# Two loads of v moved from GpSimd's DMA queue to SyncE's, each cut into 119 and 9 rows

## The chip, the cores and the metric

The kernel runs on one core of a Trainium2 chip. The metric is device time in microseconds (us), the median of several runs; lower is better. The profile comes from one further execution of the same program.

## The reference

The kernel computes two layers in one launch. The first is attention with a forget gate, over 8 batches and 8 heads, with 576 positions and 64 channels a head. The second mixes the result along the sequence in the frequency domain.

```python
# attention, for each batch and head
cum    = cumsum(log(clip(f, 0.0001, 1)))
scores = q @ k.T / sqrt(64) + cum[:, None] - cum[None, :]      # causal
x      = softmax(scores) @ v                                   # -> [8, 576, 512]
# spectral mix: 64 low modes, for each a complex 512 x 512 weight
X = rfft(x, axis=1)
Yr, Yi = Xr @ w_r - Xi @ w_i,  Xr @ w_i + Xi @ w_r             # per mode m < 64
u   = x + irfft(Y)
out = u + relu(u @ w_ch)
```

The two weights `w_r` and `w_i` are [64, 512, 512] in float32 and make up most of what is read: 134.2 MB of the 163.7 MB that the profile counts as read from HBM.

## The kernel before

**Attention stage.** Heads are taken in pairs of one batch: 32 pairs, and the list `pairs` runs over the batches inside each pair of heads. The loop at L552 runs over `i` from 0 to 33. In iteration `i` it issues loads for later pairs, computes the scores of pair `i`, and finishes the attention of pair `i - 1` and the transform (`dft`) of pair `i - 2`. From iteration 10 on it also does a part of the spectral product (`spec_early`).

**Spectral stage.** The loop at L716 runs over `u` from 0 to 15, four modes at a time. For each `u` it multiplies with the remaining weight tiles (`spec_mms`, matmuls at L194), rearranges the result, and in the later turns folds finished modes back into x (`fold_modes`, `fold`). The last `u` is multiplied in `spec_cols` (L211). Then come twenty output blocks (`bases`, `rest`) with stores from SyncE (L860 and L865).

**Loads.** Almost every load is issued by GpSimd, in program order, onto one DMA queue (q0 in the profile):

- `load_qk` (L109): q and k of a pair, cast from float32 to bf16 by the DMA, two transfers.
- `load_v` (L119): v of a pair, 128 rows of 2304 bytes in float32, with no cast, into a tile `vt` from a pool of four buffers. Row p of the tile holds nine positions of one head.
- `issue_w` (L156 and L165): weight tiles, cast to bf16, in transfers of 512 KB or 1024 KB as written. In the attention loop they are issued in halves (`issue_half`), and a pool of seven buffers (`wpool`) holds them.

In iteration `i` GpSimd issues q and k of pair `i + 4`, half a weight tile, v of pair `i + 3`, and in most iterations another half. SyncE's queue (q1 in the profile) carries only f and v of the first three pairs at the start, and the output stores at the end. The tile `vt` is read by one VectorE instruction, `scale_v` (L372), which multiplies it by the decay weights `wn`; `scale_v(i + 1)` stands near the end of iteration `i`. With four buffers, the load of v of pair 8 waits for `scale_v(4)`, and that of pair 16 for `scale_v(12)`.

The instructions themselves are fetched by DMA while the kernel runs. These fetches are the queues q8 and q14 in the profile.

Of the kernel before, what the change touches and what calls it, by code (L numbers as in the profile page):

```python
# [23 lines left out]
def kernel(  # L24
# [11 lines left out]
    nc = tc.nc  # L36
# [66 lines left out]
    def load_qk(i):  # L103
        g, b = pairs[i]
        qk = qkpool.tile([128, 2, S], BF16, tag="qk", name="qk")
        st[i]["qk"] = qk

        for n, src in enumerate((q, k)):
            nc.gpsimd.dma_start(  # L109
                qk[64 * n : 64 * n + 64, :, :],  # L110
                src[b, 2 * g : 2 * g + 2, :, :].rearrange("h (p r) d -> p h (r d)", p=64),
            )

    def load_v(i, eng=None):

        g, b = pairs[i]
        vt = vpool.tile([128, 9, Dh], F32, tag="vt", name="vt")
        st[i]["vt"] = vt
        (eng or nc.gpsimd).dma_start(  # L119
            vt[:].rearrange("p r d -> p (r d)"),  # L120
            v[b, 2 * g : 2 * g + 2, :, :].rearrange("h (c r) d -> (h c) (r d)", r=9),
        )


    early = [(u, 0) for u in range(NU)] + [(u, 1) for u in range(NX)]
# [48 lines left out]
    def issue_half():  # L174
        issue_w(whalf[0])
        whalf[0] ^= 1
# [91 lines left out]
    def setup_cum():  # L268
        nc.vector.tensor_tensor_scan(cum[:, 0:S], ones1, lf, 0.0, ALU.mult, ALU.add)
        rref = ssb.tile([BH, 1], F32, name="rref")  # L270
        nc.vector.tensor_copy(rref[:], cum[:, 256:257])
        nc.vector.tensor_scalar(cum[:, 0:S], cum[:, 0:S], rref[:], None, ALU.subtract)
        nc.vector.tensor_copy(cum[:, S : 2 * S], cum[:, 0:S])
        nc.vector.tensor_copy(cum[:, 2 * S : 2 * S + 64], cum[:, 512:576])
# [14 lines left out]
    def setup_wn(r0, r1):  # L289
        cpn = psM.tile([128, 5, BH], F32, tag="m", name="cpn")  # L290
        for r in range(r0, r1):
            nc.tensor.transpose(
                cpn[:, r - r0, :], cum[:, r : 2 * S : 9], ident_f[:BH, :BH]
            )
        for hp in range(2):
            half = slice(64 * hp, 64 * hp + 64)
            nc.scalar.activation(
                wn[half, :, r0:r1],
                cpn[half, 0 : r1 - r0, hp:BH:2].rearrange("p r w -> p w r"),
                ACT.Exp,  # L300
                scale=-1.0,
            )

    def setup_small():
        nc.vector.tensor_scalar(trimask[:], m_f[:], s_f[:, 0:1], None, ALU.is_ge)
        nc.vector.memset(tri4[:], 0.0)
        nc.vector.tensor_copy(tri4[0:64, 0, :], trimask[0:64, 0:64])
        nc.vector.tensor_copy(tri4[64:128, 1, :], trimask[64:128, 64:128])
# [37 lines left out]
    def trans(i, part):  # L346

        qk = st[i]["qk"]
        if part == 0:
            st[i]["T"] = qtkt.tile([128, 2, S], BF16, tag="T", name="qkT")  # L350
        r0, r1 = (0, 5) if part == 0 else (5, 9)
        tp = psM.tile([128, 5, 2, 64], BF16, tag="m", name="tp")
        for r in range(r0, r1):
            for hp in range(2):
                nc.tensor.transpose(  # L355
                    tp[64 * hp : 64 * hp + 64, r - r0, :, :].rearrange("p n c -> p (n c)"),
                    qk[:, hp, r * 64 : r * 64 + 64],
                    ident_bf[:, :],
                )
        nc.vector.tensor_copy(  # L360
            st[i]["T"][:].rearrange("p n (c r) -> p n c r", r=9)[:, :, :, r0:r1],
            tp[:, 0 : r1 - r0, :, :].rearrange("p r n c -> p n c r"),
        )
# [12 lines left out]
    def turn_v(i):  # L376

        tv = psM.tile([128, 9, 64], BF16, tag="m", name="tv")
        for r in range(9):
            for hp in range(2):  # L380
                sl = slice(64 * hp, 64 * hp + 64)
                nc.tensor.transpose(tv[sl, r, :], st[i]["vn"][sl, r, :], ident_bf[sl, sl])  # L382
        st[i]["vT"] = vTpool.tile([128, S], BF16, tag="vT", name="vT")
        nc.vector.tensor_copy(  # L384
            st[i]["vT"][:].rearrange("p (c r) -> p c r", r=9), tv[:].rearrange("p r c -> p c r")
        )
# [25 lines left out]
    def scores(i, T):  # L412

        QT, KT = st[i]["T"][:, 0, :], st[i]["T"][:, 1, :]
        if T == 0:
            st[i]["et"] = epool.tile([128, 3, 2, 512], BF16, tag="et", name="et")
            st[i]["e4"] = epool.tile([128, 64], BF16, tag="e4", name="e4")
            st[i]["m4"] = epool.tile([128, 2, 64], BF16, tag="m4", name="m4")
        if T == 3:
            ps = psM.tile([128, 64], F32, tag="m", name="s4")  # L420
            for hp in range(2):
                sl = slice(64 * hp, 64 * hp + 64)
                nc.tensor.matmul(
                    ps[sl, :], lhsT=KT[sl, 512:576], rhs=QT[sl, 512:576], start=True, stop=True
                )
            nc.scalar.activation(st[i]["e4"][:], ps[:], ACT.Exp, scale=scale)
            return
        ps = psS.tile([128, 2, 512], F32, tag="S", name="sps")
        for jb, i0, n, c in SPANS[T]:
            for hp in range(2):  # L430
                sl = slice(64 * hp, 64 * hp + 64)
                nc.tensor.matmul(  # L432
                    ps[:, hp, c : c + n],
                    lhsT=KT[sl, jb * 128 : jb * 128 + 128],
                    rhs=QT[sl, i0 : i0 + n],
                    start=True,
                    stop=True,
                )
        nc.scalar.activation(st[i]["et"][:, T, :, :], ps[:], ACT.Exp, scale=scale)  # L439
# [29 lines left out]
    def av(i, sb):  # L469
        if sb in (0, 3):  # L470
            st[i]["pav"] = psV.tile([128, 3, 2, Dh + 1], F32, tag="av", name="pav")
        pav, vs = st[i]["pav"], st[i]["vs"]
        Ms = SBLK[sb]
        for hp in range(2):
            for jb in range(sb + 1):
                rhs = vs[:, 8, :] if jb == 4 else vs[:, 2 * jb + hp, :]
                nc.tensor.matmul(  # L477
                    pav[:Ms, sb % 3, hp, :],
                    lhsT=eblk(i, hp, jb, sb),
                    rhs=rhs,  # L480
                    start=(jb == 0),
                    stop=(jb == sb),
                )
# [62 lines left out]
            nc.vector.tensor_tensor(y, A[:], y, ALU.add)  # L546

    less = (3, 6, 9, 12, 15)
    trans(0, 0)
    trans(0, 1)  # L550
    spec_done = 0
    for i in range(NPAIR + 2):  # L552
        live = i < NPAIR
        if i + 4 < NPAIR:
            load_qk(i + 4)
        issue_half()
        if i + 3 < NPAIR:
            load_v(i + 3)
        if i not in less:
            issue_half()  # L560
        prev = i - 1 if 1 <= i <= NPAIR else None
        if live:
            scores(i, 0)
        if i == 0:
            setup_cum()
            setup_small()
        if prev is not None:
            av(prev, 0)
            av(prev, 1)
        if live:  # L570
            scores(i, 1)
        if 0 < i < NPAIR:
            turn_v(i)
        if prev is not None:
            av(prev, 2)
            norm(prev, 0)
        if i + 1 < NPAIR:
            trans(i + 1, 0)
        if live:
            scores(i, 2)  # L580
            if i == 0:
                setup_wn(0, 5)
                setup_wn(5, 9)
                scale_v(0)
                setup_w()
                turn_v(0)
            mask(i, 0)
        if prev is not None:
            av(prev, 3)
        if i + 1 < NPAIR:  # L590
            trans(i + 1, 1)
        if live:
            scores(i, 3)
            back_v(i)
        if prev is not None:
            av(prev, 4)
            norm(prev, 1)
        if live:
            mask(i, 1)
        if i + 1 < NPAIR:  # L600
            scale_v(i + 1)
        if i == 1:
            setup_basis()
        if 10 <= i < 14:
            spec_early(*early[spec_done])
            spec_done += 1
        if i >= 2:
            dft(i - 2)
        if i == 2:
            setup_late()  # L610
        if 3 <= i < 3 + NSB:
            setup_bi(i - 3)
        if i == 3 + NSB:
            setup_bi4(0, 512)
        if i == 4 + NSB:
            setup_bi4(512, 64)
        if i >= 10:
            spec_early(*early[spec_done])
            spec_done += 1
# [3 lines left out]
    with ExitStack() as bctx:  # L623
# [8 lines left out]
        with ExitStack() as mctx:  # L632
# [83 lines left out]
            for u in range(NU):  # L716
# [4 lines left out]
                for dc in range(first, NEB - 1 if last else NEB):  # L721
# [3 lines left out]
                    if u >= NF and dc < 3:  # L725
                        b = 2 * (u - NF) + dc - 1
# [169 lines left out]
```

## Time and profile before

| What | Value |
|---|---|
| Median of 3 runs | 441.06 us (440.43 to 441.65) |
| Time of the profiled execution | 442.7 us |
| Its span, first to last instruction | 440.7 us |
| Mean granted TensorE clock | 0.936 of full speed |
| Busy: TensorE, VectorE, ScalarE, GpSimd | 344.5, 268.4, 233.3, 129.7 us |
| Read from HBM, written | 163.73 MB, 9.44 MB |
| DMA queue of GpSimd (q0) | 62800 packets, 85.64 MB as written |
| DMA queue of SyncE (q1) | 5504 packets, 10.47 MB |

The span is what the profile's rows add up to; 2.0 us of the profiled execution's time lie outside it. Busy time of an engine is an average over stages with different limits, so a change in one stage is read from that stage.

A transfer is shared out over the core's 16 DMA engines, and each of them tells of its own share's landing; whoever waits for the transfer waits for all of them. The trace keeps these landings, and it keeps every packet with its queue, start, duration and size, but not the number of the DMA engine that moved it.

### The profile page before, as it was taken

The page shows a single profiled execution, that of the slowest core. Times are in us where ns is not written, and L with a number is a line of the kernel's source. Part 1 is how long each engine was busy: PE and PEld are TensorE (multiplying, and loading weights), DVE is VectorE, ACT ScalarE, POOL GpSimd, SP SyncE. Part 2 cuts the span into 40 slices and gives each one's busy share as a digit, 9 for nine tenths or more (in the row PEclk, how much of TensorE's full clock was granted, in tenths as well). Part 3 has the DMA queues.
Part 4 walks back from the last instruction along what each step waited for, and adds up shares of the span by engine and source line. Part 5 has one row for each costly group of instructions (what it writes and reads, how often), then busy time and mean ns, then how long its engine had stood idle before and what let it go on. Part 6 is the DMA issues. An engine that isn't in the chain of part 4 may idle for free.

```text
span 440.7 us, 10287 instructions
## 1 busy us (share of the span) xinstructions
PE 344.5 (78%) x4295; PEld 189.9 (43%) x4305; DVE 268.4 (61%) x641; ACT 233.3 (53%) x355; POOL 129.7 (29%) x199
## 2 busy tenths in 40 slices
PE   1678878889889889898893694797885788979993
PEld 0455555555555565555551241343442233325331
DVE  6678888777887778888871221223231356635885
ACT  4567678778787665665640031132222355734673
POOL 6544444453454444444222111012211221100000
PEclk9999999999999999999997598599989699969997
DMA  8999999999999999999999999999999999992698
GB/s 190 205 234 221 230 220 231 232 228 227 231 231 222 231 222 229 221 230 224 232 212 212 212 212 212 212 212 212 211 212 210 211 210 210 210 210 53 219 347 294
DMA packets 68349, 96.75 MB, mean 220 GB/s; under 512 B 3536, under 2 KB 45008, under 8 KB 68304
## 3 DMA queue, kind: packets, MB, share of 16 engines
q0 software_dynamic: 62800, 85.64, 104.9%
q1 hardware_dynamic: 5504, 10.47, 6.8%
q8 instruction: 33, 0.54, 0.4%
q14 instruction: 12, 0.10, 0.1%
HBM read 163.73 MB, written 9.44 MB: 393 GB/s over the span
## 4 chain that ended last, share of the span: by engine, by line
DMA 39%; PE 34%; DVE 19%; ACT 3%; issue 3%; POOL 1%; DVEq 0%; POOLq 0%; ACTq 0%
DMA w<-in_moe_w_i_dram 22%; DMA w<-in_moe_w_r_dram 15%; DVE vT L384 5%; DVE x_all L492 4%; DVE qkT L360 4%; PE pav L477 4%; PE A L194 4%; PE sps L432 3%; PE tv L382 3%; PE pd L521 3%; PE vp L393 2%; PE U L785 2%; DMA qk<-in_k_dram 2%; PE Z L785 2%; DVE vn L372 2%
## 5 line engine op out<-in xcount | busy, mean ns | idle before, releaser
L439 ACT ACTIVATE et<-sps 128x1024 bf16<-128x1024 f32 x96 | 96.0, 1050 | 12.6 <-PE sps L432 10.2
L744 DVE TENSOR_TENSOR Yb<-A,yx 128x512 bf16<-128x512 f32 x15 | 10.4, 692 | 67.6 <-PE A L194 67.6
L477 PE MATMUL pav<-vs,et 128*128 128x65 bf16 (+1 forms) x896 | 51.2, 197 | 0.2 <-DVE vn L372 0.2
L360 DVE COPY qkT<-tp 128x640 bf16<-128x640 bf16 x64 | 48.8, 763 | 3.1 <-PE tp L355 3.0
L477 PEld LDWEIGHTS <-et 128*128 128x128 bf16 (+1 forms) x896 | 36.5, 102 | 17.2 <-issue 13.3
L194 PE MATMUL A<-w,XP 128*16 128x512 bf16 (+1 forms) x240 | 22.6, 457 | 27.1 <-DMA w<-in_moe_w_i_dram 15.6
L660 PE MATMUL pxw<-wch,xT 128*128 128x512 bf16 (+1 forms) x152 | 39.1, 403 | 1.0 <-DVE xT L651 0.4
L432 PE MATMUL sps<-qkT 64*128 64x512 bf16 (+4 forms) x320 | 38.9, 306 | 1.1 <-DVE qkT L360 1.1
L492 DVE TENSOR_TENSOR x_all<-pav,rcp 128x384 bf16<-128x384 f32 (+2 forms) x96 | 36.2, 377 | 3.3
L355 PE MATMUL tp<-ident_bf,qk 128*64 128x128 bf16 x576 | 29.3, 231 | 9.9 <-DMA qk<-in_k_dram 9.9
L384 DVE COPY vT<-tv 128x576 bf16<-128x576 bf16 x32 | 24.2, 757 | 19.3 <-PE tv L382 19.3
L667 ACT CAST XW<-pxw 128x512 bf16<-128x512 f32 (+1 forms) x15 | 8.8, 585 | 48.3 <-PE pxw L660 48.3
L165 POOL DMA_DIRECT2D w<-in_moe_w_r_dram x16 | 11.9, 743 | 70.1 <-PE A L194 56.7
L404 ACT COPY vs<-vp 128x576 bf16<-128x576 bf16 x32 | 20.5, 640 | 21.4 <-PE vp L400 21.4
L156 POOL DMA_DIRECT2D w<-in_moe_w_r_dram x27 | 20.5, 759 | 38.5 <-PE A L194 8.6
L667 ACT CAST yx<-pxw 128x512 bf16<-128x512 f32 (+1 forms) x25 | 14.6, 585 | 32.4 <-PE pxw L660 32.4
L165 POOL DMA_DIRECT2D w<-in_moe_w_i_dram x19 | 13.3, 700 | 55.8 <-PE A L194 26.1
L109 POOL DMA_DIRECT2D qk<-in_q_dram x32 | 19.7, 614 | 33.8 <-PE tp L355 7.8
L706 ACT CAST x_all<-pu 128x512 bf16<-128x512 f32 (+1 forms) x40 | 23.4, 584 | 9.0 <-PE pu L705 8.0
L491 DVE RECIPROCAL rcp<-pav 128x6 f32<-128x6 f32 (+2 forms) x96 | 16.2, 169 | 16.3 <-PE pav L477 16.1
L156 POOL DMA_DIRECT2D w<-in_moe_w_i_dram x27 | 20.4, 756 | 17.5 <-DMA w<-in_moe_w_i_dram 8.2
L109 POOL DMA_DIRECT2D qk<-in_k_dram x32 | 19.4, 605 | 20.2 <-DMA w<-in_moe_w_r_dram 6.5
(134 smaller groups left out, 666.5 us busy)
## 6 DMA issues: line engine op xcount, KB each, us to landing
w<-in_moe_w_r_dram POOLq DMA_DIRECT2D x16, 1024.0 KB, 29.6
w<-in_moe_w_i_dram POOLq DMA_DIRECT2D x15, 1024.0 KB, 32.1
w<-in_moe_w_r_dram POOLq DMA_DIRECT2D x27, 512.0 KB, 11.1
w<-in_moe_w_i_dram POOLq DMA_DIRECT2D x27, 512.0 KB, 12.5
vt<-in_v_dram POOLq DMA_DIRECT2D x29, 288.0 KB, 10.6
out_dram<-o_sb SPq DMA_DIRECT2D x16, 512.0 KB, 3.4
qk<-in_q_dram POOLq DMA_DIRECT2D x32, 144.0 KB, 10.7
qk<-in_k_dram POOLq DMA_DIRECT2D x32, 144.0 KB, 10.8
```

The costliest lines, as they stand in the source:

```text
L109: nc.gpsimd.dma_start(qk[64 * n : 64 * n + 64, :, :], src[b, 2 * g : 2 * g + 2, :, :].rearrange("h (p r) d -> p h (r d)", p=64),)
L156: nc.gpsimd.dma_start(w8[:, t, :, :], src[4 * u : 4 * u + 4, dc * 128 : (dc + 1) * 128, :].rearrange("m p e -> p m e"),)
L165: nc.gpsimd.dma_start(w8[:, j : j + step, :, :].rearrange("p m r e -> p m (r e)"), src[m : m + step, 256:512, :].rearrange("m (p r) e -> p ...
L194: nc.tensor.matmul(A[32 * j : 32 * j + M, :], lhsT=lhsT, rhs=rhs, start=st_, stop=sp_)
L355: nc.tensor.transpose(tp[64 * hp : 64 * hp + 64, r - r0, :, :].rearrange("p n c -> p (n c)"), qk[:, hp, r * 64 : r * 64 + 64], ident_bf[:, :],
L360: nc.vector.tensor_copy(st[i]["T"][:].rearrange("p n (c r) -> p n c r", r=9)[:, :, :, r0:r1], tp[:, 0 : r1 - r0, :, :].rearrange("p r n c ...
L384: nc.vector.tensor_copy(st[i]["vT"][:].rearrange("p (c r) -> p c r", r=9), tv[:].rearrange("p r c -> p c r"))
L432: nc.tensor.matmul(ps[:, hp, c : c + n], lhsT=KT[sl, jb * 128 : jb * 128 + 128], rhs=QT[sl, i0 : i0 + n], start=True, stop=True,)
L439: nc.scalar.activation(st[i]["et"][:, T, :, :], ps[:], ACT.Exp, scale=scale)
L477: nc.tensor.matmul(pav[:Ms, sb % 3, hp, :], lhsT=eblk(i, hp, jb, sb), rhs=rhs, start=(jb == 0), stop=(jb == sb),)
L492: nc.vector.tensor_tensor(x_all[:ns, g, b, lo:hi, :].rearrange("p s (h d) -> p s h d", h=2), pav[:ns, lo % 3 : lo % 3 + n, :, 0:Dh], _stri ...
L660: nc.tensor.matmul(pxw[:Ms, :], lhsT=xT[:, eb, sb * 128 : sb * 128 + Ms], rhs=wch[:, eb, :], start=(eb == 0), stop=(eb == NEB - 1),)
```

## The change

In iterations 5 and 13, v of pairs 8 and 16 (the ninth and the seventeenth) is loaded by two transfers on SyncE's queue, of rows 0 to 118 and of rows 119 to 127, instead of one transfer of 128 rows on GpSimd's queue. The other 27 loads of v in the loop stay as they are. The bytes, the tile and its reader are the same.

```diff
-    def load_v(i, eng=None):
+    def load_v(i, eng=None, parts=((0, 128),)):
 
         g, b = pairs[i]
         vt = vpool.tile([128, 9, Dh], F32, tag="vt", name="vt")
         st[i]["vt"] = vt
-        (eng or nc.gpsimd).dma_start(
-            vt[:].rearrange("p r d -> p (r d)"),
-            v[b, 2 * g : 2 * g + 2, :, :].rearrange("h (c r) d -> (h c) (r d)", r=9),
-        )
+        rows = v[b, 2 * g : 2 * g + 2, :, :].rearrange("h (c r) d -> (h c) (r d)", r=9)
+        for p0, p1 in parts:
+            (eng or nc.gpsimd).dma_start(
+                vt[p0:p1, :, :].rearrange("p r d -> p (r d)"), rows[p0:p1, :]
+            )
...
     less = (3, 6, 9, 12, 15)
+    uneven = (8, 16)
...
         if i + 3 < NPAIR:
-            load_v(i + 3)
+            if i + 3 in uneven:
+                load_v(i + 3, nc.sync, ((0, 119), (119, 128)))
+            else:
+                load_v(i + 3)
```

## The prediction

> **What bounds the kernel now.** I read the slices and queues of the page first, then the chain, then TensorE's timeline where the chain changes hands, and last the rows of `vt`.
>
> ```profile
> DMA  8999999999999999999999999999999999992698
> ...
> q0 software_dynamic: 62800, 85.64, 104.9%
> q1 hardware_dynamic: 5504, 10.47, 6.8%
> q8 instruction: 33, 0.54, 0.4%
> q14 instruction: 12, 0.10, 0.1%
> ...
> DMA 39%; PE 34%; DVE 19%; ACT 3%; issue 3%; POOL 1%; DVEq 0%; POOLq 0%; ACTq 0%
> ```
>
> The DMA engines are over 90% busy in every slice up to about 397 us, whatever the compute engines do, and DMA holds the largest share of the chain. So the loads run as one stream, and the kernel ends a fixed tail after that stream. The chain's order of time (rows from 309 us, three of them) and TensorE's timeline show where the tail begins:
>
> ```profile
> 309.21 33.62 DMA w<-in_moe_w_i_dram
> ...
> 359.39 28.41 DMA w<-in_moe_w_i_dram
> 387.84 1.09 PE A L194 x7
> ```
>
> ```profile
> 385.26 0.65 PE L194 MATMUL A<-w,XP 128*16 128x512 bf16 x8
> 387.84 1.06 PE L194 MATMUL A<-w,XP 128*16 128x512 bf16 x8 [1.93 <-DMA w<-in_moe_w_i_dram]
> ```
>
> The chain goes over for good from DMA to TensorE at 387.84 us, when the last weight tile of `u` = 14 has landed (387.80). TensorE had waited 1.93 us for it. The later tiles land before TensorE comes to them (the last at 402.90, used at 405.03), so the end lies 52.9 us after this one landing.
>
> A landing means the last of 16 shares. The landing records of this tile, one per DMA engine, lie at these lags after the first, in us: 0, 0.09, 0.38, 0.50, 0.51, 1.64, 2.45, 2.84, 2.98, 3.91, 4.02, 4.16, 4.86, 4.89, 4.96, 5.92. Each engine gets an equal share of every transfer before, so the lags are work of other kinds. The instruction fetches are that work: q8 has 33 of 16 KB, each one packet on one engine, of 0.89 to 0.98 us (one longer), and where one falls after 220 us, the lag of one engine grows by about 1 us and the others stay (at the landing after the fetch of 255.7 us the last lag goes from 5.02 to 5.97). The fetches come round to the same engine every eighth time (223.0 and 399.6 us), and the eight engines that they visit are, as far as the records can be followed, the eight slowest in the list. Smaller fetches (q14, 0.32 us) explain part of the middle. Fast engines do not wait for slow ones: the queue is 10 to 30 us deep (median from issue to landing 10.6 us for v, 29.6 us for the large weight tiles). The kernel is therefore bound by its slowest DMA engine, 5.92 us behind the fastest and 1 us behind the next.
>
> **The change, part by part.**
>
> *Removed from GpSimd's queue:* two transfers. The rows of v:
>
> ```profile
> L372 DVE TENSOR_TENSOR vn<-vt,wn x32: 741/743/758, 17.6 to 221.7; 128x576 bf16<-128x576 f32 x32
> L119 POOL DMA_DIRECT2D vt<-in_v_dram x29: 557/562/578, 16.4 to 207.9; - x29
> L119 SPq DMA_DIRECT2D vt<-in_v_dram x3: 432/432/560, 1.4 to 2.5; - x3
> ```
>
> GpSimd saves 2 x 0.562 us of issue. That is worth nothing: what follows in its order is queued 1.7 to 23 us before the first engine gets to it. Every DMA engine loses its share of 8 rows, which takes 0.73 us (step from one landing to the next on the first engine, 0.71 to 0.75 where nothing disturbs it). Twice: 1.46 us.
>
> *Added to SyncE's queue:* four transfers of about 0.43 us of issue each, on an engine with nothing between 3 us and the stores at 410.5 us; nothing is queued behind them that matters. They wait for the buffer: `scale_v(4)` ends at 42.9 us and `scale_v(12)` at 94.3 us, against issues on GpSimd at 52.1 and 104.5 us. So v comes some 10 us earlier than now and is read at 67.6 and 120.8 us; a landing even 10 us slower than now is hidden. VectorE's two `scale_v` wait for two landings each instead of one, at a cost of 0.02 us (its one separate semaphore step takes 21 ns), within gaps of that engine.
>
> *The shares.* The trace shows only transfers of 64 and 128 rows on SyncE's queue, and each lands in 16 steps. 119 is 7 x 17 and 9 is 3 x 3, so neither divides by 16. Equal shares mean at most seven engines of 17 rows, and nine of one row. A row of 2304 bytes on this queue takes 0.093 us alone (median packet). Back to back, packets start 0.089 us apart. The seven engines then carry 18 x 0.089 = 1.60 us in place of 0.73, which is +0.87 us each time and +1.74 in all. Engines that get nothing gain 1.46; those with one row gain 1.46 - 0.18 = 1.28. Mixing two queues on an engine may cost more: in the first 10 us, where both run, the same packets often take 0.106 us, 0.013 more. 36 of these are +0.47, so the seven's price lies between +1.74 and +2.21. I take 1.74, from rows in their steady run, and keep the other for the range.
>
> The trace does not say which seven. The Trainium skill, page "DMA: Bandwidth & Descriptors", section "Why a DMA increments its semaphore by 16 and not by 1", says that on this queue the largest count up to 16 that divides the row dimension is used, on the lowest-numbered engines. That gives engines 0 to 6 for the 119 rows; no run so far shows a transfer that doesn't divide by 16.
>
> A hint from packet records: an output store at 413.27 us coincides with the last q8 fetch. Its first packets start on 15 engines 0 to 154 ns after the first, at nearly the same distances as in the store before; the one missing is, in that store, about the twelfth of 16 to start. If shares are handed out in engine order, the fetched engines are not the first seven. This is weak, but it is all there is.
>
> *The sum.* If the seven are among the engines without q8 fetches, the slowest goes from 5.92 to 5.92 - 1.46 = 4.46, and the highest of the others from 2.84 to 2.84 + 1.74 = 4.58. The new last share is at 4.46 to 4.58: 1.34 to 1.46 us earlier, less than TensorE's wait of 1.93, so the whole tail moves. The span becomes 440.7 - 1.4 = 439.3, and the profiled execution 442.7 - 1.4 = 441.3. That execution lies 1.6 us above the median of the runs; I carry the difference over, which gives 441.06 - 1.4 = 439.7 us (0.3% less). With mixing, 2.84 + 2.21 = 5.05, and the gain is 0.87.
>
> **Rivals.**
>
> *The seven include the laggards (slower).* Place: the landing at 387.80. If the engine at 5.92 is among the seven, it goes to 5.92 + 1.74 to 2.21, and the end moves to 442.8 to 443.3 us. If only the one at 4.96 is, 4.96 + 1.74 = 6.70, and the end is 0.8 later, 441.8. It decides as soon as any engine above 5.92 - 1.74 = 4.18 is loaded, and four are. For it: eight of 16 engines are visited, and seven drawn blindly would nearly always hit one of the four. Against: the hint above, and fetches that keep to eight engines look like a fixed half.
>
> *The shares aren't equal but spread over all 16,* 7 or 8 rows each. Then the queue changes and no engine's load does: 8 x 0.089 = 0.71 against 0.73. 441.0 us. All 16 landings of 64 and 128 rows speak for it as much as for the forecast.
>
> *Few engines.* Were all 119 rows on one, 119 x 0.089 = 10.6 us each time, 21.2 in all on one engine, less 1.46: even the fastest would end 13.8 us after the slowest now, near 455 us. Nothing in the trace speaks for it.
>
> The Trainium skill has a rule against the change: the same page, "Rules for kernel authors", asks for a dimension that is a multiple of 16 outermost, so that all 16 engines work. By it the transfer itself takes longer, 17 rows or 1.5 us for 0.73; here that is hidden 10 us deep, and only the sum per engine counts.
>
> **How the numbers follow.** A measurement of this kernel tells about 0.3% (1.3 us) from no change. Equal shares on engines without q8 fetches: 0.67, of which 0.53 beyond 0.3% and 0.14 below (mixing). Laggards among the seven: 0.25, of which 0.22 beyond. Spread: 0.05, same. Few engines: 0.03, slower. That is faster 0.53, same 0.22, slower 0.25. The prediction is 439.7. The range starts at the gain of 1.46 with 0.4 for the spread of runs, 439.2, and reaches up into the laggard case, 442.9; on its own the likeliest case has 439.2 to 440.4.
>
> **What would show it.** Right: q1 gains 256 rows (0.59 MB) and one landing packet for each share, so 5504 + 256 + 32 = 5792 packets if seven and nine engines take part and 5824 if all 16 do; the lags of the last tiles spread over 4.5 us instead of 5.9; the chain's hand-over to TensorE comes near 386.4 with a wait of about 0.5 us. Wrong: a hand-over after 387.8 with a spread of 6.7 or more (laggards loaded), or a spread of 5.9 unchanged (spread shares). A landing of v later than 67.6 or 120.8 us would refute that its time is hidden.

## The result, and the profile after

The changed kernel takes 444.12 us (median of 6 runs, 442.81 to 445.41), the kernel before 441.0 us in the same job (median of 6, 440.0 to 443.26). The ratio is 1.0062, 95% interval 1.0039 to 1.0086: 2.7 us slower by this ratio (the medians lie 3.1 us apart), where the forecast was 1.4 us faster. A second job (run `e11_after_again` below) gave 1.0060 (1.0032 to 1.0088).

The page of the changed kernel, the slices, queues and shares of the chain:

```profile
DMA  8999999999999999999999999999999999993697
...
q0 software_dynamic: 62640, 85.05, 104.7%
q1 hardware_dynamic: 5792, 11.06, 7.2%
q8 instruction: 34, 0.56, 0.5%
q14 instruction: 12, 0.10, 0.1%
...
DMA 39%; PE 36%; DVE 17%; ACT 4%; issue 2%; POOL 1%; DVEq 0%; POOLq 0%; ACTq 0%
```

The DMA engines are as busy as before. q1 has the 5792 packets that the prediction gave for shares on seven and on nine engines, and not the 5824 of shares on all 16. The Trainium skill's rule for that (page "DMA: Bandwidth & Descriptors", section "Why a DMA increments its semaphore by 16 and not by 1": the largest number up to 16 that divides the rows) agrees with this count.

The rows of v, and the chain where it goes over from DMA to TensorE, with TensorE's timeline there:

```profile
L373 DVE TENSOR_TENSOR vn<-vt,wn x32: 741/743/759, 17.2 to 223.7; 128x576 bf16<-128x576 f32 x32
L121 POOL DMA_DIRECT2D vt<-in_v_dram x27: 562/562/571, 16.5 to 210.7; - x27
L121 SPq DMA_DIRECT2D vt<-in_v_dram x7: 270/350/560, 1.4 to 96.6; - x7
```

```profile
311.90 33.64 DMA w<-in_moe_w_i_dram
...
361.69 28.82 DMA w<-in_moe_w_i_dram
390.55 0.67 PE A L195 x8
```

```profile
389.12 0.64 PE L195 MATMUL A<-w,XP 128*16 128x512 bf16 x8
390.55 0.65 PE L195 MATMUL A<-w,XP 128*16 128x512 bf16 x8 [0.79 <-DMA w<-in_moe_w_i_dram]
```

The hand-over is at 390.55 us; it was at 387.84 and was expected at 386.4. The last weight tile lands from 399.52 us (first of 16 shares) to 405.54 (last share), before from 396.93 to 402.90. So both ends of the stream came 2.6 us later, and the spread stayed at 6.0 us.

The span of this execution grew by 1.0 us alone (441.7 for 440.7). In it TensorE had a higher granted clock behind the hand-over, which fits a shorter tail. Two rows of the table of stretches, first of the changed kernel, then of the kernel before (columns: stretch, its length, TensorE busy, granted clock, DMA share, GB/s):

```profile
388.00:400.00 12.00, 9.89 (x90) 1.00 1.14 208
```

```profile
388.00:400.00 12.00, 10.91 (x79) 0.73 1.03 190
```

The clock was 1.00 in the one and 0.73 in the other, and the tail from the hand-over to the end took 51.2 us in the one and 52.9 in the other. One execution's span can therefore hide a shift of the stream; I read shifts from the landings, and times from the medians.

### The profile page after: what moved, and what is told of

The parts are those of the page before. It is cut to its first block, busy times and chain, and to the rows that moved or that the text cites. A ratio compares the mean times of both kernels' runs of the same rounds, so it can differ in the third digit from the quotient of the medians.

```text
span 441.7 us, 10310 instructions
## 1 busy us (share of the span) xinstructions
PE 351.4 (80%) x4305; PEld 192.8 (44%) x4305; DVE 269.4 (61%) x641; ACT 233.2 (53%) x355; POOL 128.6 (29%) x197
## 3 DMA queue, kind: packets, MB, share of 16 engines
q1 hardware_dynamic: 5792, 11.06, 7.2%
## 4 chain that ended last, share of the span: by engine, by line
DMA 39%; PE 36%; DVE 17%; ACT 4%; issue 2%; POOL 1%; DVEq 0%; POOLq 0%; ACTq 0%
DMA w<-in_moe_w_i_dram 22%; DMA w<-in_moe_w_r_dram 15%; PE pav L478 5%; DVE vT L385 4%; DVE qkT L361 4%; DVE x_all L493 4%; PE A L195 4%; PE sps L433 3%; PE tv L383 3%; PE pd L522 3%; PE vp L394 2%; PE U L790 2%; DMA qk<-in_k_dram 2%; PE Z L790 2%; ACT e L427 1%
## 5 line engine op out<-in xcount | busy, mean ns | idle before, releaser
L478 PE MATMUL pav<-vs,et 128*128 128x65 bf16 (+1 forms) x896 | 52.7, 200 | 0.2 <-DVE vn L373 0.2
L478 PEld LDWEIGHTS <-et 128*128 128x128 bf16 (+1 forms) x896 | 37.6, 104 | 18.3 <-issue 13.8
L665 PE MATMUL pxw<-wch,xT 128*128 128x512 bf16 (+1 forms) x160 | 41.9, 419 | 0.0
L433 PE MATMUL sps<-qkT 64*128 64x512 bf16 (+4 forms) x320 | 40.5, 317 | 1.1 <-DVE qkT L361 1.1
L356 PE MATMUL tp<-ident_bf,qk 128*64 128x128 bf16 x576 | 30.3, 237 | 9.6 <-DMA qk<-in_k_dram 9.6
L166 POOL DMA_DIRECT2D w<-in_moe_w_i_dram x19 | 13.3, 700 | 57.0 <-PE A L195 26.2
L665 PEld LDWEIGHTS <-xT 128*128 128x128 bf16 (+1 forms) x160 | 15.8, 108 | 22.7 <-issue 9.2
```

What stands on the lines that cost most here:

```text
L166: nc.gpsimd.dma_start(w8[:, j : j + step, :, :].rearrange("p m r e -> p m (r e)"), src[m : m + step, 256:512, :].rearrange("m (p r) e -> p ...
L356: nc.tensor.transpose(tp[64 * hp : 64 * hp + 64, r - r0, :, :].rearrange("p n c -> p (n c)"), qk[:, hp, r * 64 : r * 64 + 64], ident_bf[:, :],
L433: nc.tensor.matmul(ps[:, hp, c : c + n], lhsT=KT[sl, jb * 128 : jb * 128 + 128], rhs=QT[sl, i0 : i0 + n], start=True, stop=True,)
L478: nc.tensor.matmul(pav[:Ms, sb % 3, hp, :], lhsT=eblk(i, hp, jb, sb), rhs=rhs, start=(jb == 0), stop=(jb == sb),)
L665: nc.tensor.matmul(pxw[:Ms, :], lhsT=xT[:, eb, sb * 128 : sb * 128 + Ms], rhs=wch[:, eb, :], start=(eb == 0), stop=(eb == NEB - 1),)
```

## The experiments

Four ideas were held against each other. *Engine sum:* the end goes with the DMA engine that has most to do, and one of the engines far behind is among the seven loaded. *Window:* GpSimd issues a transfer only after the eighth one before it has landed whole, so late shares hold up all engines. *Queue:* v on SyncE's queue comes too early or costs as such. *The forecast's sum:* the seven are engines without large instruction fetches, and nobody waits for them. ("Lane theory" in the texts on record is the engine sum in its first form; the "price theory" of the last run is the engine sum with the row prices of the traces.)

The window came from the trace. In the landing records, GpSimd's transfers use eight semaphores in turn. The issue of transfer n is never less than 0.284 us after the last share of transfer n - 8; in the attention stage 68 of some 140 issues, before as after, lie within 0.5 us of it. GpSimd's timeline after and before, around the first uneven load:

```profile
51.56 0.60 POOL L109 DMA_DIRECT2D qk<-in_k_dram  x1 [3.62 <-DMA yx<-in_moe_w_i_dram]
```

```profile
49.63 0.60 POOL L109 DMA_DIRECT2D qk<-in_k_dram  x1 [1.70 <-DMA yx<-in_moe_w_i_dram]
```

The same wait is 1.9 us longer: that weight tile's last share came at 51.27 us in place of 49.34.

The window holds up engines that are ahead, not the one that is behind. In every run, from 20 us on, the last share of a transfer of GpSimd's lands 7.0 us or more after the next transfer was issued. So the slowest engine has 7 us of work or more in its queue whenever GpSimd goes on, and that speaks against the window as the cause of a later end.

All results in one table. Time: ratio to the kernel before in the same job, its 95% interval, and the shift at 441 us. Landings: first and last share of the last weight tile in the one profiled execution, against the kernel before (396.93 and 402.90 us).

| Run | Ratio (95%) | Time, us | First share, us | Last share, us |
|---|---|---|---|---|
| the change | 1.0062 (1.0039-1.0086) | +2.7 | +2.6 | +2.6 |
| e1_one128 | 0.9998 (0.9977-1.0019) | -0.1 | +0.9 | +1.0 |
| e2_gp_split | 0.9989 (0.9969-1.0009) | -0.5 | -0.6 | -0.3 |
| e3_late | 1.0031 (1.0012-1.0049) | +1.4 | +1.0 | +1.1 |
| e4_four | 1.0139 (1.0100-1.0177) | +6.1 | +6.5 | +6.0 |
| e5_probe_att | 1.0054 (1.0034-1.0074) | +2.4 | +3.1 | +3.3 |
| e6_probe_spec | 1.0045 (1.0028-1.0062) | +2.0 | -0.05 | +3.4 |
| e8_allv | 1.0061 (1.0044-1.0078) | +2.7 | +2.9 | +2.3 |
| e9_allv_uneven | 1.0082 (1.0065-1.0098) | +3.6 | +1.8 | +3.8 |
| e10_six | 1.0176 (1.0128-1.0225) | +7.8 | -0.6 | +8.6 |
| e11_after_again | 1.0060 (1.0032-1.0088) | +2.6 | +2.5 | +2.9 |
| e12_five | 1.0035 (1.0014-1.0055) | +1.5 | +2.9 | +2.4 |
| e13_12_20 | 1.0062 (1.0035-1.0089) | +2.7 | +2.0 | +1.6 |

### Is it the uneven shares or the queue? (e1_one128, e2_gp_split)

```diff
 e1:  load_v(i + 3, nc.sync)                          # one transfer of 128 rows on SyncE's queue
 e2:  load_v(i + 3, None, ((0, 119), (119, 128)))     # two transfers, on GpSimd's queue
```

Expected of the first: 

> v of pairs 8 and 16 on SyncE's queue as one transfer of 128 rows, so that all 16 DMA engines carry equal shares; queue and early issue as in the changed kernel. Window theory (GpSimd issues its transfer n only after the last share of transfer n-8 has landed; uneven shares make that last share late): no uneven shares, so the time of the kernel before, 440.5 to 441.5 us, and the last landings stay within 0.5 us of its. Lane theory (the seven engines end as the slowest): the same. Queue theory (v jumps ahead of q, k and the weights some 10 us early, and this costs): as slow as the changed kernel, 443 to 445 us.

Expected of the second: 

> v of pairs 8 and 16 stays on GpSimd's queue at its own time, but in transfers of 119 and 9 rows. If GpSimd's queue hands out the rows as SyncE's does (seven and nine engines), the window theory and the lane theory both give 443 to 445 us, the queue theory 441. If it spreads 119 rows over all 16 engines, window and lane theory give 441.0 to 442.0 (two more issues of 0.6 us, and two more places taken in the row of eight); queue theory 441.

Neither costs anything that can be measured. The first has the early issue, SyncE's queue and GpSimd's two transfers less, and is as fast as before, so the queue theory falls for two transfers. Its profile shows the stream 1.0 us late, but the profiled execution was the longest of its 12 runs (443.25 us, median 442.11): a shift of this size in one execution proves nothing. In the second, GpSimd's queue moved the 119 rows in 59 packets of two rows and one of one row: eight rows for an engine, as with 128 (in the landing records of pair 16, 15 of the 16 engines take a share). So the loss belongs to the shares that SyncE's queue makes of 119 rows.

### Dose and place (e4_four, e3_late, e13_12_20, e12_five, e11_after_again)

```diff
 e4:  uneven = (8, 12, 16, 20)
 e3:  uneven = (28, 31)
 e13: uneven = (12, 20)
 e12: load_v(i + 3, nc.sync, ((0, 125), (125, 128)))  # for pairs 8 and 16
 e11: no edit, the changed kernel again
```

Expected of e4: 

> v of pairs 8, 12, 16 and 20 in transfers of 119 and 9 rows on SyncE's queue: the dose doubled. Window theory: each uneven transfer holds up the stream by about what the slowest engine has more, so about twice the loss, 446 to 448 us. Lane theory with the seven as the engines without large fetches: they end at 2.84 + 4 x 0.87 = 6.3 against 5.92 of the slowest before, at most +0.4: 441.5, and with mixing 443.3. Noise of the one profile: nothing can be said, but the loss would not double.

Expected of e3: 

> The uneven transfers on SyncE's queue are those of pairs 28 and 31 in place of 8 and 16: the same number of bytes on the same engines, but issued near 165 and 190 us, with only two to five v transfers left behind them. Window theory: the stream still waits on the last share for the rest of the attention stage, but the number of issues that lie at the window's edge is small, so 0 to 1.5 us later than before: 441.0 to 442.5. Lane theory with the seven as the slow ones: the whole +1.7 to 2.2 and more, 443 to 445. The forecast's sum (the seven are the engines without large instruction fetches, and nothing waits for a late share): 439.6 to 440.2.

Expected of e12: 

> v of pairs 8 and 16 in 125 and 3 rows, so five engines of 25 rows (with one more on three of them). Engine-sum theory: 26 x 0.106 - 0.73 = +2.03 on the most loaded, twice +4.1: 445 if one of the slowest is among the five; if the slowest are outside, and the five are at most 2.98 behind, +1.1 at most: 442. Mere count of uneven transfers (two, as in the change): +2.7, 443.7.

Expected of e11: 

> The changed kernel itself, unaltered, for a second profile and a tighter interval. Engine-sum theory (the end goes with the engine that has most to do; a row of 2304 bytes costs 0.106 us on SyncE's queue, a loaded engine carries 18 such rows and loses 0.73 each time): 2 x (1.91 - 0.73) = +2.4 us at the last landing. Window theory as the cause of the end: +2.7 as before, without a reason for just that number. Both near 443.7, so this run is for the size.

Expected of e13, the last run: 

> The uneven transfers are those of pairs 12 and 20 in place of 8 and 16. In the kernel with four of them the rows of these two took 0.105 and 0.109 us (mean packet), where the rows of pair 8 in the changed kernel take 0.146 to 0.160. Price theory (part of the loss is that the rows of pair 8 are dear): 2 x (18 x 0.107 - 0.73) = +2.4 on the loaded engines in place of +3.3, less the 1.0 that the slowest of the seven is behind the slowest of all: +1.0 to +1.7 in time, 442 to 443 for a kernel before at 441. If two uneven transfers cost the same wherever they stand in the attention stage: +2.7.

Four uneven transfers cost 6.1 us, 1.5 for each, where two cost 2.7. Here v itself comes late as well, which the waits of VectorE in the attention stage from 160 us on show (engine, tile, line, what it waited for: us in total, times, longest). The kernel before has no such wait, and the change has one, of 0.3 us.

```profile
DVE vn L373 <- DMA vt<-in_v_dram: 6.7, 7, 1.5
```

With pairs 28 and 31 the loss is 1.4 us (0.5 to 2.2), against 2.7 (1.7 to 3.8) for the change. The window theory had expected this (0 to 1.5), and the doubled loss of e4 too; the engine sum had expected more from e3 (+2 to +4) and gave no reason for less. The intervals overlap, so that the late place costs less is not shown by the times. Pairs 12 and 20 cost 2.7 again (1.5 to 3.9), where the dearer rows of pair 8 were to explain 1 us: that explanation isn't borne out by the times. (In e13 the rows of pair 12 took 0.106 us, those of pair 20 0.127; its last share moved by 1.6.) Five engines with 26 rows on three of them, instead of seven with 18, cost 1.5 and not 4.1: the most loaded engines are not always the ones that matter. If the five are among the seven, which no run shows, one slow engine would be the sixth or seventh. That was not tried by itself.

### Does the window set the end? (e5_probe_att, e6_probe_spec)

Both leave every load of the kernel before as it is and add two writes of 119 rows to a spare tensor on SyncE's queue; only the place differs.

```diff
+ spare = [nc.dram_tensor(f"spare{n}", (128, 9 * Dh), F32, kind="Internal").ap() for n in range(2)]
+ def dump(n, tile_, rows):
+     nc.sync.dma_start(spare[n][0:rows, :], tile_[0:rows, :, :].rearrange("p r d -> p (r d)"))
 e5, after load_v(i + 3), for pairs 8 and 16:   + dump((i + 3) // 8 - 1, st[i + 3]["vt"], 119)
 e6, after Yb, for u = 2 and 4:                 + nc.vector.memset(scr[:], 0.0); dump(u // 2 - 1, scr, 119)
```

Expected of e5: 

> The kernel before with nothing moved; as soon as v of pair 8 and of pair 16 has landed, SyncE writes 119 rows of it (2304 bytes each) to a spare DRAM tensor that nobody reads. This adds 17 rows to seven DMA engines, twice, and nothing to the others. Window theory: the seven are 1.6 us later each time (more if mixing costs), GpSimd's eighth transfer after it is issued later, and the whole stream shifts: +2 to +4 us, 443 to 445, with the first landing of the last tile later by nearly as much as its last landing. Forecast's sum (fast engines do not wait; the seven are the ones without large instruction fetches): only the seven move, from 2.84 to 6.0 at most, +0.1 us, first landing unmoved. Lane theory with the seven as laggards: +3.2 at the last landing, first landing unmoved.

Expected of e6: 

> The same two writes of 119 rows, but in the spectral stage (at u = 2 and u = 4, from a tile of zeros), where GpSimd has issued 18 to 23 us ahead and waits for no landing. Window theory: nothing in front of the queue is held up, the first landing of the last tile stays; only the seven move by 1.6 us each time. If they are the engines without large fetches, they come from at most 2.84 to about 6.0: 441.0 to 442.0. If they hold the laggards, 5.92 becomes 9.1: 444. So this run tells which engines the seven are, and whether the place of the uneven load matters.

This pair settles the main question. In the attention stage GpSimd is held, and the first share comes 3.1 us later. GpSimd's timeline of e5, after the second write:

```profile
123.93 0.60 POOL L110 DMA_DIRECT2D qk<-in_k_dram  x1 [2.39 <-DMA w<-in_moe_w_i_dram]
```

The same issue in the kernel before:

```profile
121.21 0.60 POOL L109 DMA_DIRECT2D qk<-in_k_dram  x1 [1.68 <-DMA w<-in_moe_w_i_dram]
```

In the spectral stage, where issue runs some 20 us ahead, the first share doesn't move (-0.05 us). (From 333 us on six issues stand at the window's edge there too, the last weight tile's among them, which is issued 3.4 us later in e6. But it still goes out 10 us before its first share lands.) Yet the last share moves by the same in both, 3.3 and 3.4 us, and the times agree within their intervals, 2.4 and 2.0 us. TensorE's hand-over in e6, with an undisturbed front:

```profile
391.28 0.66 PE L198 MATMUL A<-w,XP 128*16 128x512 bf16 x8 [0.71 <-DMA w<-in_moe_w_i_dram]
```

So the window is real and makes fast engines wait, but the end goes with the slowest engine, which has work queued all the time. And e6 refutes the forecast's choice: 2 x 17 x 0.106 = 3.6 us on engines that are at most 2.84 behind would have ended at 6.4, +0.5 us; the lag of the last share became 9.4. Followed from landing to landing, that engine is one of the seven: it was 4.9 behind the first before the writes, moved 3.4 us by them, and 1.1 by the large fetch (q8) at 285 us.

The landing records of e6 also give the price of a row. Each write of 17 rows moves the seven by about 1.70 us, 0.100 a row. The packets last 0.106 us, but packets overlap (the four queues of the page add up to over 100% of the 16 engines' span), so sums of their durations come out too high.

### Which engines are the seven? (e10_six)

```diff
-                if u in (2, 4):        # e6
+                if u < 6:              # six writes, u = 0 to 5
```

Expected: 

> Six writes of 119 rows from a tile of zeros in the spectral stage (u = 0 to 5) in place of two, nothing else changed. At 17 x 0.106 = 1.80 us each, the seven loaded engines move 10.8 us behind where they were, so the 16 landings of the last tile must fall into two groups, and the lags of the loaded group less 10.8 are their lags without it. If the seven are the engines without large fetches (the forecast), the loaded group ends at 2.98 + 10.8 = 13.8 at most, about +7.8 us, and no large fetch after 300 us raises a lag in it. If they hold the slowest (the rival), it ends at 5.9 + 10.8 = 16.7 or little less, +10 to +11 us, and some fetches raise lags in the loaded group.

The 16 landing records fall into two groups. Lags after the first, in us, ahead of the writes (tile that lands from 232.2 us), after the last of them (296.7), and at the end (396.3):

```
232.2:  0 .04 .12 .24 .61 .63 .82 2.42 3.43 3.48 3.74 3.81 3.95 4.51 4.99 5.52
296.7:  0 .16 .69 3.39 3.63 3.71 5.41 5.50 5.96 | 10.18 10.22 10.81 11.14 12.55 13.60 14.11
396.3:  0 .13 .70 3.62 4.47 4.78 5.41 5.50 5.98 | 10.14 10.19 10.83 11.09 13.04 14.62 15.14
```

Seven engines left the other nine. The lowest of them lies 10.14 to 10.18 us behind the first of all, which is about 102 rows at 0.100. Taking 10.15 us off, they lie at 0.0, 0.1, 0.7, 1.0, 2.4, 3.4 and 4.0: four near the front and three well behind it. The top two of the group rise by 1.08 and 1.07 us, in the landings right behind the large fetches (q8) at 312 and 333 us; engines of the other nine rise by 1.0 to 1.1 behind those at 289, 363 and 386 us. So the fetches visit engines of both groups. The slowest of the seven would have ended at 15.14 - 10.15 = 5.0, 1 us less than the slowest of the nine (5.98). In e6 and in e10 the large fetches that raise a lag of the seven are those whose packet took 0.89 us, and the others followed took 0.94 to 0.97. In the kernel before, the two of 0.89 us after 300 us raise the lags that end at 4.86 and 3.91. So the engine at 4.86 was probably the slowest of the seven there; that is inferred from the packets' lengths, as the trace has no engine numbers. TensorE shows the cost:

```profile
396.48 0.65 PE L198 MATMUL A<-w,XP 128*16 128x512 bf16 x8 [1.95 <-DMA w<-in_moe_w_i_dram]
```

The hand-over is 8.6 us later than before, the time 7.8 us (two runs, 5.6 to 9.9); the first share came 0.6 us *earlier*. The time is the number that was expected if the forecast's choice held, so it decides nothing. What speaks against that choice are the fetches that hit the loaded group, and its last lag of 15.1 where at most 13.8 was allowed. It lies between the two expectations because the slowest of the seven is not the slowest of all.

### The change in a kernel with a longer window (e8_allv, e9_allv_uneven)

```diff
 e8:  load_v(i + 3, nc.sync)                                   # every pair, 128 rows
 e9:  the same, but pairs 8 and 16 as ((0, 119), (119, 128))
```

Expected of e8: 

> v of every pair from the fourth on goes on SyncE's queue in one transfer of 128 rows; none is uneven. GpSimd's row of eight then holds only weights, q and k, so it reaches some 20% further in time. Window theory: the edge of the window is reached less often; the time is that of before or up to 1 us less, 440 to 441.5. Queue theory (v on SyncE as such costs): 29 transfers in place of 2 would show it, well over 443.

Expected of e9: 

> As the kernel with all v on SyncE's queue, but v of pairs 8 and 16 in 119 and 9 rows, so the change made in a kernel whose window reaches further. Window theory: less than the +2.7 us that the change cost in the kernel before, +0.5 to +1.8 over its partner with all v even. Lane theory: the whole +2.7.

All v on SyncE's queue, evenly, costs 2.7 us. That is against the window theory (up to 1 us less) and with the queue theory (over 443 us): v on SyncE's queue does cost as such, but little for each transfer. The page gives the number of packets: q0 loses 2320 packets and q1 gains 4176.

```profile
q0 software_dynamic: 60480, 77.08, 99.4%
q1 hardware_dynamic: 9680, 19.03, 12.6%
```

GpSimd's queue moves v in packets of two rows (4608 bytes, a step of 0.73 us for eight rows), SyncE's in packets of one row, 0.106 us each: 8 x 0.106 = 0.85. The 0.12 more, times 29 transfers, makes 3.4 us on every engine; at 0.100 a row it is 2.0. The last share came 2.3 us later, which is 0.101 a row. For two transfers it is at most 0.24 us, too small to see in e1. On top of that the uneven shares cost 0.9 us in time, with intervals that overlap, and 1.5 at the last share (10 rows more, twice, at 0.100 to 0.12: 2.0 to 2.4). The first share came 1.0 us earlier than in e8. The window theory's expectation (0.5 to 1.8) held, and the engine sum's (2.7) did not. Part of the difference is that the partner pays SyncE's price already; whether that is all of it isn't shown.

## Why the prediction was wrong, point by point

- **The bound was right.** Time follows the last share in the table and not the first (e6 and e10 against e5). The tail behind the hand-over was not quite fixed: 50.7 us in e6, 51.2 after the change, 52.9 before.
- **The shares were right:** 5792 packets, and 5776 in e12 (five and three engines).
- **"If the seven are among the engines without q8 fetches" failed.** At least two of the seven are visited by the large fetches (e10), and the slowest of the seven is about 1 us or less short of the slowest of all (e6, e10). The order of packet starts in one output store, which the prediction called weak, was the only ground. The rival "the seven include the laggards" is what happened, on its own terms: any loaded engine above 4.18 decides, and the one at 4.86 was probably loaded. By the prediction's row prices that one would give +0.7 to +1.15 us at the last share; the rest needs the next point.
- **The row's price was mis-sized.** The term was 18 x 0.089 = 1.60 us. In e6 and e10 a row cost 0.100 (written; read, 0.101 in e8), inside the range that the prediction kept for mixing (0.102). But the packets of these loads took 0.146 and 0.106 us on the mean (0.160 and 0.109 in e11), so 18 x (0.146 + 0.106) = 4.5 us for the two, less 1.46 removed, is +3.1 where the prediction had +1.74 to 2.21. With the slowest of the seven up to 1 us short of the slowest of all, that gives +2.1 to +3.1 at the last share; measured +2.6 and +2.9. At 0.100 a row it would be +1.1 to +2.1, too little. The rival's end of 443.3 us falls short by this term.
- **"Fast engines do not wait", because "the queue is 10 to 30 us deep", was false, and did not set the time.** Depth in time was the wrong measure; GpSimd looks back eight transfers. What it did spoil was my test: a spread that stays at 5.9 was to mean shares on all 16 engines. The spread stayed at 6.0 because the fast engines were held back in the attention stage. In e6 and e10, loaded where the first share isn't held back, it grew to 9.4 and 15.1.
- **The hidden parts were hidden.** GpSimd's saved issues and the earlier v changed nothing that can be measured (e1). The last rows of the two loads started at 52.9 and 103.4 us. `scale_v` of pairs 8 and 16 started at 69.5 and 122.7 us behind VectorE's own work, with no wait for v in its timeline.
- **The rule against the change** (the Trainium skill, "DMA: Bandwidth & Descriptors", "Rules for kernel authors": a multiple of 16 outermost) did hold in its result: two such transfers cost 2.7 us, four 6.1 us.

What stays open is the size, to about 1 us. By their packets' durations e3, e12 and e13 should have moved the last share by 2.7, 5.3 and 2.7 us, and it moved by 1.1, 2.4 and 1.6. At 0.100 a row it would be 2.1, 3.7 and 2.1, less up to 1 us for the seven's distance: that fits e3 and e13 and comes near e12, but it is too little for the change, and for e4 (4.3, measured 6.0, with v late). So no single price fits all runs. When a fetch hits a loaded engine differs from one profiled execution to the next, and one execution of each can't tell. No version here beats the kernel before; e1 and e2 can't be told from it.

## What to carry to other kernels

When a stream of loads sets the end, add up the work of each DMA engine and look at the last share of each landing: an uneven transfer can cost about what it adds to an engine that is far behind, even if its own latency is hidden and even if it stands where issue is not held up. Unless a run shows which engines a transfer uses and that they are the idle ones, keep rows on SyncE's queue a multiple of 16; a few extra copies of the transfer, as in e10, set its engines apart in the landing records. To tell a late front from a late last share, put the same load once where the queue is held and once where it runs far ahead.

## What the runs showed of the hardware

- The packet of a row of 2304 bytes lasts 0.106 us on SyncE's queue beside GpSimd's casts, in reads (e8) and writes (e6) alike, and costs its engine 0.100 (landings of e6 and e10). In the changed kernel, when seven engines took pair 8's rows at 48 to 53 us, it lasted 0.146 to 0.160 on the mean; in e4 and e9 the same rows lasted 0.127 and 0.123, and pair 20's in e13 0.127. With the same rows of pair 8 on all 16 engines at the same place it was 0.105. The cause was not tried.
- In e6 the seven engines start seven SyncE packets in every 0.25 us, so each engine does one SyncE packet (0.100) and about 0.15 us of GpSimd's work in turn, and 17 rows spread over 4.2 us while they cost 1.7. That agrees with the Trainium skill, "DMA: Bandwidth & Descriptors", section "Queues, rings and completion order", by which an engine takes a packet from each queue in turn.
- The same 119 rows go to seven engines from SyncE and, eight rows at a time, to nearly all from GpSimd (e2).
